# Turning a convolution filter by whole transposes with half-zero tables in a fused gated mixer kernel

## The chip, the core and the metric

The kernel runs on one core of a Trainium2 chip. The metric is the device time of one execution in microseconds (us); the median over the runs is given, with the lowest and the highest. Engines are named as in the profile: PE is TensorE (matmul, and PEld its weight loads), DVE is VectorE, ACT is ScalarE, POOL is GpSimd, and SP issues most DMA transfers.

## The reference

All inputs are bf16; the length S is 2048 and the width D is 640. Two branches of x (which is also q) are mixed by a gate:

```python
def _A_ref(q, k, v, shift_k, ssm_k, ssm_D):      # q, k, v: (1, 2048, 640)
    k_shift = sum over t of k_pad[:, t:t + S, :] * shift_k[:, 3 - t]     # 4 taps
    kv = k_shift * v
    y = irfft(rfft(kv padded to 4096) * rfft(ssm_k padded to 4096))[:2048]
    y = y + kv * ssm_D
    return q * y

def _B_ref(x, w1, w2, w3, w4):
    h = gelu(layernorm(x) @ w1)                  # 640 -> 640
    hs = (four column groups of h, moved by +1, -1, +2, -2 rows) @ w2
    x1 = x + hs
    return x1 + gelu(layernorm(x1) @ w3) @ w4    # 640 -> 1536 -> 640

g = sigmoid((x * gate_w).sum(-1))
return g * _A_ref(x, ...) + (1 - g) * _B_ref(x, ...)
```

## The kernel before

Time is tiled into 16 blocks of 128 rows (NT), the width into 5 blocks of 128 columns (DC). The long convolution is a Fourier transform of length 4096, done in steps of small matmuls against sine tables that the kernel computes itself.

*Branch A.* k is loaded (k_load, `kn`), turned by PE (L571, tile `pst`) and convolved with the four taps by matmuls (tap, L543, tile `psk`). v is gathered by row with indirect DMAs that POOL issues (v_load, L150, four chunks of four blocks, v3 to v0). DVE multiplies both into `KV` (L557 straight from PSUM, L554 from an ACT copy). The filter ssm_k (640 x 2048) is loaded with channels on partitions (load_h, L163, tiles `E` and `HN`) and has to be turned so that time lies on partitions: h_transpose (L343 to L361) does that with PE transposes (L352), two of 128 x 64 for each 128 x 128 tile, one for the even rows of an order "(t2 r t1)" and one for the odd ones (r), at the two column positions of the array. In such a transpose the filter tile is the weight of the matmul, so that its strided view is what PE loads as weights (PEld). One evacuation per 8 tiles writes the turned filter, HT0.

step1 (L378) is the first step of the transform, for KV and for HT0: 4 chunks of 5 units, each unit two matmuls against table F1, one on partitions 0 to 63 and one on 64 to 127 (row positions 0 and 64), 512 columns each. Each unit leaves two PSUM banks, which ACT or DVE copies to `stg` (evac, L325 on ACT and L327 on DVE); SP sends them to DRAM (S_x for KV, S_h for the filter). gather (L396) reads them back in the order of the next step; step2 (L417) does it, product multiplies the two spectra on DVE, step3 (L464) goes back, its results `gs` travel through DRAM (S_g) and gin (L489), and step4 (L829) ends the transform. The gated mix with q (L836, L839) and with branch B (L843) is done there.

*Branch B.* x_stats (L621 and on: DVE statistics at L638, POOL's power at L610 for the reciprocal root, L611) and x_norm (L617) normalise; mlp1 (L663, tile `psm`), h_shift, w2 (L740), x1_norm with a transposing DMA (L767), w3 (L788) and w4 (L806, L808) are the two perceptrons.

*Order.* Nothing is left to a scheduler: a list ORDER of steps (name, arguments, number of the step) is written out by hand, and each engine and queue gets its instructions in that order. Letters in an entry (AAVAAAAVAA) say for each evacuation whether ACT (A) or DVE (V) does it. PSUM banks with tag "c" rotate through 4 buffers, staging rows (tag "row") through 4. warm (L198 to L202) runs 11 matmuls on zeros at the very start. f1_table, f4_table, t2_table and i_tables make the sine tables on DVE with one ACT sine each (L240 to L242).

Of the kernel before, what the change touches and what calls it, by code (L numbers as in the profile page):

```python
# [41 lines left out]
def kernel(  # L42
# [38 lines left out]

    ROWS = const.tile([P, 1], I32, name="ROWS")
    WZ = const.tile([P, 512], BF16, name="WZ")
    IDB = const.tile([P, P], BF16, name="IDB")
    F1 = const.tile([P, H, 2], BF16, name="F1")
    F4 = const.tile([P, 2, H, 2], BF16, name="F4")
# [52 lines left out]
    def col(i):  # L139
        return sm[:, i:i + 1]  # L140
# [57 lines left out]
    def warm():  # L198
        V.memset(WZ[:], 0.0)
        ps = psc.tile([P, 512], F32, name="psz", tag="c")  # L200
        for i in range(11):
            PE.matmul(ps[:], lhsT=WZ[:, 0:P], rhs=WZ[:], start=True, stop=True)  # L202

# [40 lines left out]
    def f1_table():  # L244


        stt(pf2[:], bit(6), -64.0, pf[:])
        ts(col(29), pf2[:], 2.0)
        n = tab([P, H, 2], "n")
        ts(n[:, :, 0], R64[:, 0:H], col(29), pf2[:])  # L250
        ts(n[:, :, 1], n[:, :, 0], float(128 + 128), op0=ALU.add)
        ts(n[:, :, 0], n[:, :, 0], float(64 + 128), op0=ALU.add)
        yield from sin_table(F1[:], n, 256)

# [85 lines left out]
    def h_transpose(dc, ev):  # L340
        if "HT0" not in st:
            st["HT0"] = main.tile([P, NT * D], BF16, name="HT0", tag="RT")
        hv = st.pop(("HN", dc)).rearrange("p (t2 r t1) -> p t1 r t2", r=2, t1=NT)  # L343
        dst = st["HT0"][:].rearrange("p (t d) -> p t d", t=NT)
        def make(hh):
            box = {}

            def first():
                ps = box["ps"] = psc.tile([P, 8, P], BF16, name="pst", tag="c")
                for i in range(8):  # L350
                    for r in range(2):
                        PE.transpose(out=ps[HALF[r], i, :], in_=hv[:, 8 * hh + i, r, :], identity=IDB[:], tile_position=(0, H * r))  # L352
# [13 lines left out]
    def step1(name, c, ev):  # L366
# [5 lines left out]
        def make(u):  # L372
            ps = []

            def first():
                for r in range(2):
                    ps.append(psc.tile([P, 512], F32, name="ps1", tag="c"))
                    PE.matmul(ps[r][:], lhsT=F1[HALF[r]].rearrange("p a b -> p (a b)"), rhs=src[HALF[r], o + 512 * u:o + 512 * u + 512], start=True, stop=True,  # L378
                              tile_position=(H * r, 0))
# [435 lines left out]
    def step4(t1, ev):  # L815
# [32 lines left out]
        "open.L1.left:0 open.A2.right:0 kv_alloc:0 warm:0 load_x0.0:0 consts0:0 load_x0.1:0 k_load.3.AAA:0 load_cj:0 "  # L848
        "consts0:1 f4_table:0 f1_table:0 k_load.1.AAV:0 k_load.2.AAA:0 f4_table:1 f1_table:1 load_x.1:0 k_load.0.AAA:0 "
        "x_stats.0.VVVA:0 x_stats.0.VVVA:1 x_stats.0.VVVA:2 x_stats.0.VVVA:3 x_stats.0.VVVA:4 row_order:0 load_w1:0 "  # L850
        "k_load.3.AAA:5 load_gw:0 k_load.3.AAA:6 k_load.3.AAA:3 k_load.3.AAA:1 k_load.1.AAV:1 k_load.1.AAV:5 "
        "x_stats.0.VVVA:5 k_load.3.AAA:4 k_load.1.AAV:3 load_x.3:0 k_load.3.AAA:2 k_load.1.AAV:2 kv_consts:0 "
        "k_load.2.AAA:3 v_load.3:0 k_load.1.AAV:4 x_stats.0.VVVA:6 x_norm.0.VVVV:0 x_norm.0.VVVV:1 x_norm.0.VVVV:2 "
        "k_load.1.AAV:6 k_load.2.AAA:1 k_load.2.AAA:4 k_load.2.AAA:2 d_fold:0 x_turn.0.VAV:0 x_norm.0.VVVV:3 "
        "x_turn.0.VAV:4 v_load.2:0 k_load.2.AAA:5 x_turn.0.VAV:1 x_turn.0.VAV:2 k_load.2.AAA:6 x_turn.0.VAV:3 "
        "x_turn.0.VAV:5 tap.7.AA:0 tap.7.AA:1 k_load.0.AAA:1 k_wrap:0 tap.9.VA:0 x_stats.1.VVVV:0 x_stats.1.VVVV:1 "
        "x_stats.1.VVVV:2 x_stats.1.VVVV:3 tap.9.VA:1 tap.7.AA:3 k_load.0.AAA:2 load_h.0:0 tap.7.AA:4 x_stats.1.VVVV:4 "
        "k_load.0.AAA:5 tap.9.VA:3 mlp1.0.1:0 tap.5.AV:0 v_load.1:0 x_stats.1.VVVV:5 tap.9.VA:2 k_load.0.AAA:6 "
        "load_x.2:0 tap.7.AA:2 tap.5.AV:3 tap.5.AV:4 mlp1.0.1:1 w1_mixed:0 tap.5.AV:1 tap.6.VA:0 tap.6.VA:1 tap.6.VA:2 "
        "tap.8.VA:0 k_load.0.AAA:3 tap.5.AV:2 mlp1.0.0:0 load_h.1:0 x_norm.1.VVVV:0 x_norm.1.VVVV:1 x_norm.1.VVVV:2 "  # L860
        "x_norm.1.VVVV:3 x_stats.3.VVAA:0 x_stats.3.VVAA:1 tap.6.VA:3 v_load.0:0 tap.8.VA:1 x_stats.3.VVAA:2 "
        "x_turn.1.AAV:4 tap.8.VA:3 x_stats.3.VVAA:3 k_load.0.AAA:4 x_turn.1.AAV:2 x_turn.1.AAV:5 x_turn.1.AAV:0 "
        "x_stats.3.VVAA:4 mlp1.0.2:0 x_stats.3.VVAA:5 x_stats.3.VVAA:6 tap.8.VA:4 x_stats.3.VVAA:7 x_turn.1.AAV:3 "
        "tap.8.VA:2 tap.4.AV:0 tap.6.VA:4 x_turn.1.AAV:1 mlp1.0.0:1 tap.4.AV:1 tap.9.VA:4 x_norm.3.VVVV:0 tap.4.AV:3 "
        "x_norm.3.VVVV:1 tap.4.AV:4 x_norm.3.VVVV:2 tap.3.AA:0 mlp1.0.2:1 x_norm.3.VVVV:3 tap.3.AA:1 mlp1.1.1:0 "
        "tap.3.AA:3 step1.KV.3.VAVAVAAAAA:0 x_stats.2.VVAA:0 step1.KV.3.VAVAVAAAAA:1 step1.KV.3.VAVAVAAAAA:6 "
        "x_stats.2.VVAA:1 x_stats.2.VVAA:2 x_stats.2.VVAA:3 step1.KV.3.VAVAVAAAAA:2 step1.KV.3.VAVAVAAAAA:7 mlp1.1.0:0 "
        "tap.3.AA:4 step1.KV.3.VAVAVAAAAA:8 x_stats.2.VVAA:4 x_stats.2.VVAA:5 tap.0.VV:0 x_stats.2.VVAA:6 x_turn.3.D:0 "
        "tap.4.AV:2 tap.0.VV:3 tap.0.VV:1 mlp1.1.0:1 load_h.3:0 tap.2.AA:0 mlp1.1.1:1 x_stats.2.VVAA:7 tap.0.VV:4 "
        "mlp1.1.2:0 tap.0.VV:2 x_norm.2.VVVA:0 tap.2.AA:3 step1.KV.3.VAVAVAAAAA:3 x_norm.2.VVVA:1 x_norm.2.VVVA:2 "  # L870
        "tap.2.AA:1 step1.KV.3.VAVAVAAAAA:4 x_norm.2.VVVA:3 h_shift.0:0 step1.KV.3.VAVAVAAAAA:5 "
        "step1.KV.3.VAVAVAAAAA:9 step1.KV.3.VAVAVAAAAA:11 mlp1.1.2:1 mlp1.3.0:0 t2_table:0 step1.KV.3.VAVAVAAAAA:10 "
        "tap.2.AA:4 step1.KV.3.VAVAVAAAAA:12 step1.KV.3.VAVAVAAAAA:13 h_shift.0:1 mlp1.3.0:1 tap.1.VV:0 mlp1.3.2:0 "
        "tap.1.VV:1 h_shift.0:2 x_turn.2.D:0 step1.KV.3.VAVAVAAAAA:14 tap.2.AA:2 step1.KV.3.VAVAVAAAAA:16 mlp1.3.1:0 "
        "step1.KV.2.VAAVVAAVAV:6 tap.1.VV:3 tap.1.VV:2 mlp1.3.2:1 step1.KV.2.VAAVVAAVAV:8 tap.1.VV:4 "
        "step1.KV.3.VAVAVAAAAA:15 tap.3.AA:2 step1.KV.2.VAAVVAAVAV:3 step1.KV.2.VAAVVAAVAV:4 t2_table:1 mlp1.2.1:0 "
        "step1.KV.2.VAAVVAAVAV:5 step1.KV.2.VAAVVAAVAV:7 step1.KV.1.AVVAVVAAVA:9 mlp1.3.1:1 step1.KV.1.AVVAVVAAVA:11 "
        "h_shift.1:0 step1.KV.1.AVVAVVAAVA:6 h_shift.0:3 step1.KV.1.AVVAVVAAVA:8 mlp1.2.2:0 step1.KV.1.AVVAVVAAVA:10 "
        "mlp1.2.1:1 load_w2:0 step1.KV.1.AVVAVVAAVA:0 step1.KV.1.AVVAVVAAVA:1 load_h.2:0 h_shift.3:0 h_shift.3:1 "
        "step1.KV.1.AVVAVVAAVA:7 z_rows:0 h_shift.1:1 step1.KV.1.AVVAVVAAVA:12 step1.KV.1.AVVAVVAAVA:2 mlp1.2.0:0 "  # L880
        "mlp1.2.2:1 z_rows:1 step1.KV.1.AVVAVVAAVA:14 step1.KV.1.AVVAVVAAVA:13 step1.KV.1.AVVAVVAAVA:3 "
        "step1.KV.1.AVVAVVAAVA:5 h_shift.3:2 z_rows:2 h_shift.2:0 step1.KV.2.VAAVVAAVAV:9 h_shift.1:2 "
        "step1.KV.1.AVVAVVAAVA:4 step1.KV.2.VAAVVAAVAV:10 w2.0:0 h_shift.2:1 step1.KV.2.VAAVVAAVAV:11 "
        "step1.KV.2.VAAVVAAVAV:0 w2.0:1 mlp1.2.0:1 step1.KV.2.VAAVVAAVAV:12 step1.KV.2.VAAVVAAVAV:13 "
        "step1.KV.2.VAAVVAAVAV:1 h_shift.2:2 w2.15:0 h_transpose.0.VV:2 h_shift.1:3 h_transpose.2.AV:2 "
        "step1.KV.2.VAAVVAAVAV:2 t2_table:2 h_transpose.1.VA:2 step1.KV.2.VAAVVAAVAV:14 h_transpose.0.VV:3 "
        "h_transpose.2.AV:3 w2.15:1 h_transpose.1.VA:0 h_transpose.2.AV:0 h_transpose.2.AV:1 h_transpose.1.VA:1 "
        "h_transpose.0.VV:0 w2.2:0 step1.KV.0.AAAAVAAAAA:0 step1.KV.1.AVVAVVAAVA:16 h_transpose.1.VA:3 "
        "step1.KV.1.AVVAVVAAVA:15 h_transpose.0.VV:1 step1.KV.0.AAAAVAAAAA:1 step1.KV.0.AAAAVAAAAA:6 h_shift.3:3 "
        "load_h.4:0 step1.KV.0.AAAAVAAAAA:8 w2.2:1 step1.KV.0.AAAAVAAAAA:7 step1.KV.0.AAAAVAAAAA:2 w2.12:0 "  # L890
        "step1.KV.0.AAAAVAAAAA:12 w2.2:2 step1.KV.2.VAAVVAAVAV:15 step1.KV.0.AAAAVAAAAA:9 step1.KV.0.AAAAVAAAAA:10 "
        "t2_table:3 t2_table:4 step1.KV.0.AAAAVAAAAA:11 w2.1:0 w2.12:1 step1.KV.0.AAAAVAAAAA:13 "
        "step1.KV.0.AAAAVAAAAA:14 step1.KV.0.AAAAVAAAAA:3 h_shift.2:3 step1.KV.0.AAAAVAAAAA:5 step1.KV.2.VAAVVAAVAV:16 "
        "step1.KV.0.AAAAVAAAAA:4 h_transpose.4.AV:0 h_transpose.4.AV:2 h_transpose.4.AV:3 h_transpose.3.AV:0 "
        "h_transpose.4.AV:1 h_transpose.3.AV:2 z_cols:0 load_w3:0 w2.1:1 h_transpose.3.AV:3 h_transpose.3.AV:1 "
# [159 lines left out]
```

## Time and profile before

| what | value |
|---|---|
| median of 3 runs (lowest to highest) | 241.19 us (241.0 to 242.49) |
| span of the profiled execution | 240.6 us |
| its mean granted TensorE clock | 0.984 |
| PE busy | 227.9 us |
| DVE busy | 193.3 us |
| ACT busy | 170.4 us |
| POOL busy | 19.1 us |
| traffic | 57.08 MB, of which 54.10 MB on SP's queue |

The span goes from the first to the last instruction of one profiled execution, so a sum made from its rows is compared with 240.6 and not with the median. In lists of groups a line reads: line of the kernel, engine, operation, output and inputs by the program's names, and the number of instructions; durations there are of single instructions, and matmuls overlap their successors. How far apart they follow each other is read from the chain of waits, whose lines are: start, length, engine and what it did, and how many instructions.

### The profile page before, as it was taken

Reading aid. Unit: us, or ns where it says so; the run is one execution under the profiler, and the core shown is the slowest. Engines: PE = TensorE matmul, PEld = TensorE weight load, DVE = VectorE, ACT = ScalarE, POOL = GpSimd, SP = SyncE. Lnnn points to the kernel's source line nnn. Section 1 sums busy time; section 2 is a strip of 40 time slices with the busy share of each in tenths; the row PEclk is TensorE's granted clock in tenths of the full one; section 3 lists DMA queues with packets and bytes.
Section 4 is the critical chain, followed back from the end, with each engine's and each line's share of the span. In section 5 each row is a group of like instructions: output and inputs, shape, how many; then the busy total and the mean of one; then the engine's idle time right before and its main releaser. Section 6 shows DMA issues by size and latency. Waiting matters only on the chain.

```text
span 240.6 us, 5764 instructions
## 1 busy us (share of the span) xinstructions
PE 227.9 (95%) x2328; PEld 117.7 (49%) x2328; DVE 193.3 (80%) x449; ACT 170.4 (71%) x303; POOL 19.1 (8%) x32
## 2 busy tenths in 40 slices
PE   6598999999999999999999999999999999989991
PEld 2585755433858445344355334444444345446660
DVE  7876999988876999756679999867688999209994
ACT  4689999779587899899577677675598533436530
POOL 3540322000000020002200300000000000000000
PEclk9689999999999999999999999999999999999999
DMA  6999608693989889994989936199830127689674
GB/s 218 389 379 417 224 2 198 163 343 121 348 302 344 207 346 277 374 385 170 291 206 271 207 121 223 34 244 392 318 110 3 48 107 259 214 301 347 147 276 165
DMA packets 42744, 57.08 MB, mean 237 GB/s; under 512 B 20313, under 2 KB 35418, under 8 KB 42462
## 3 DMA queue, kind: packets, MB, share of 16 engines
q1 hardware_dynamic: 42142, 54.10, 68.5%
q0 software_dynamic: 576, 2.62, 2.9%
q8 instruction: 18, 0.29, 0.5%
q14 instruction: 8, 0.07, 0.1%
HBM read 34.42 MB, written 18.36 MB: 219 GB/s over the span
## 4 chain that ended last, share of the span: by engine, by line
PE 74%; DMA 13%; DVE 9%; POOL 2%; issue 1%; SPq 0%; DVEq 0%
PE ps L788 20%; PE ps L806 15%; PE psw L740 10%; PE psm L663 8%; PE ps L378 5%; PE ps L417 4%; DMA KV<-in_A_v_dram,ROWS 4%; PE pst L352 4%; PE ps L464 3%; PE psk L543 3%; DMA ax<-S_h 2%; DMA q<-in_A_q_dram 2%; DMA gin<-S_g 2%; DVE X L843 2%; DVE q L839 2%; POOL RS L610 2%
## 5 line engine op out<-in xcount | busy, mean ns | idle before, releaser
L806 PE MATMUL ps<-W,gt 128*128 128x512 bf16 (+1 forms) x384 | 56.6, 300 | 0.0
L788 PE MATMUL ps<-x1t,W 128*128 128x512 bf16 x240 | 55.6, 380 | 0.0
L806 PEld LDWEIGHTS <-gt 128*128 128x128 bf16 x384 | 29.0, 98 | 24.9 <-issue 4.6
L788 PEld LDWEIGHTS <-W 128*128 128x128 bf16 x240 | 21.8, 98 | 29.2 <-issue 5.6
L325 ACT CAST stg<-ps 128x512 bf16<-128x512 f32 x51 | 27.3, 597 | 6.7 <-PE ps L378 5.8
L793 ACT ACTIVATE gt<-ps 128x1024 bf16<-128x1024 f32 x24 | 24.8, 1031 | 6.4 <-PE ps L788 6.1
L325 ACT CAST gs<-ps 128x320 bf16<-128x320 f32 x36 | 13.9, 431 | 16.7 <-PE ps L464 11.7
L663 PE MATMUL psm<-xt,WA 128*128 128x512 bf16 x100 | 23.5, 380 | 0.0
L740 PE MATMUL psw<-WA,HT 128*128 128x512 bf16 (+1 forms) x116 | 21.5, 300 | 0.0
L327 DVE CAST stg<-ps 128x512 bf16<-128x512 f32 x29 | 19.3, 683 | 2.5 <-PE ps L378 1.9
L325 ACT CAST hs<-ps 128x512 bf16<-128x512 f32 x28 | 15.2, 591 | 8.3 <-PE ps L417 8.2
L327 DVE CAST gs<-ps 128x320 bf16<-128x320 f32 x28 | 12.7, 485 | 5.6 <-PE ps L464 3.8
L833 ACT ACTIVATE y<-ps,GS 128x320 bf16<-128x320 f32 x19 | 9.7, 526 | 10.0 <-PE ps L829 8.5
L327 DVE CAST XS<-ps 128x512 bf16<-128x512 f32 x18 | 11.8, 684 | 5.7 <-PE ps L417 5.7
L808 DVE SCALAR_TENSOR_TENSOR X<-ps,OMG,X 128x640 bf16<-128x640 f32 x16 | 14.0, 877 | 1.7 <-PE ps L806 1.7
L839 DVE SCALAR_TENSOR_TENSOR q<-ps,GS,q 128x320 bf16<-128x320 f32 x13 | 7.1, 546 | 9.7 <-PE ps L829 9.7
L325 ACT CAST XS<-ps 128x512 bf16<-128x512 f32 x22 | 11.9, 593 | 4.0 <-PE ps L417 3.7
L740 PEld LDWEIGHTS <-HT 128*128 128x128 bf16 x116 | 9.3, 98 | 11.2 <-issue 3.0
L663 PEld LDWEIGHTS <-WA 128*128 128x128 bf16 x100 | 9.0, 98 | 11.5 <-issue 1.6
L742 DVE SCALAR_TENSOR_TENSOR X<-psw,X 128x640 bf16<-128x640 f32 x16 | 12.9, 818 | 0.9 <-PE psw L740 0.7
L417 PE MATMUL ps<-ax,CMP 64*32 64x512 bf16 (+3 forms) x512 | 13.0, 300 | 0.5 <-DMA ax<-S_h 0.5
L745 ACT ACTIVATE jk<-X 128x640 bf16<-128x640 bf16 x16 | 12.0, 751 | 0.0
(141 smaller groups left out, 356.0 us busy)
## 6 DMA issues: line engine op xcount, KB each, us to landing
S_x<-stg SPq DMA_DIRECT2D x8, 640.0 KB
ax<-S_x SPq DMA_DIRECT2D x8, 640.0 KB
S_h<-stg SPq DMA_DIRECT2D x8, 640.0 KB
ax<-S_h SPq DMA_DIRECT2D x8, 640.0 KB
S_g<-gs SPq DMA_DIRECT2D x8, 640.0 KB
W<-in_B_w_dram SPq DMA_DIRECT2D x2, 1920.0 KB
kn<-in_A_k_dram SPq DMA_DIRECT2D x4, 640.0 KB
q<-in_A_q_dram SPq DMA_DIRECT2D x4, 640.0 KB
```

The costliest lines, as they stand in the source:

```text
L325: A.copy(out=dst, in_=src)
L327: V.tensor_copy(out=dst, in_=src)
L378: PE.matmul(ps[r][:], lhsT=F1[HALF[r]].rearrange("p a b -> p (a b)"), rhs=src[HALF[r], o + 512 * u:o + 512 * u + 512], start=True, stop=Tr ...
L417: PE.matmul(ps[j][q:q + 32, lo - 512 * u:hi - 512 * u], lhsT=CMP[HALF[j], 8 * b + 4 * h + i, c, :], rhs=st[name, 2 * b + h][HALF[j], i, lo ...
L663: PE.matmul(ps[:, v, :].rearrange("p (a b) -> p a b", a=4), lhsT=W1N[:, k, 160 * f:160 * f + P] if f < 4 else W1M[:, k, :], rhs=xt[:, :, k ...
L740: PE.matmul(ps[:, o:o + w], lhsT=h_tile(f, t1), rhs=W2P[:, f, o:o + w], start=(f == 0), stop=(f == 4))
L742: V.scalar_tensor_tensor(out=X1[:, t1, :], in0=ps[:], scalar=1.0, in1=X[:, t1, :], op0=ALU.mult, op1=ALU.add, accum_out=S12[:, 0, t1:t1 + 1])
L745: A.activation(out=jk[:], in_=X1[:, t1, :], func=ACT.Square, accum_out=S12[:, 1, t1:t1 + 1])
L788: PE.matmul(ps[:, u, :].rearrange("p (a b) -> p a b", a=4), lhsT=st["W3"][:, k, f * P:(f + 1) * P], rhs=xt[:, :, k, :], start=(k == 0), st ...
L793: A.activation(out=gt[:, 2 * (fp % 2):2 * (fp % 2) + 2, :], in_=ps[:], func=ACT.Gelu_apprx_tanh)
L806: PE.matmul(ps[:, o:o + w], lhsT=st["gt", c, f // 4][:, f % 4, i * P:(i + 1) * P], rhs=st["W4"][:, f, o:o + w], start=(f == 0), stop=(f == ...
L808: V.scalar_tensor_tensor(out=X1[:, t1, :], in0=ps[:], scalar=OMG[:, t1:t1 + 1], in1=X1[:, t1, :], op0=ALU.mult, op1=ALU.add)
```

## The change

1. h_transpose reads the filter in plain row order, "(q t1)", and turns each 128 x 128 tile with one whole transpose: 80 instead of 160.
2. For HT0, step1 uses full 128-row matmuls with a new table F1N, which has two versions: one with the odd rows' entries zero and one with the even rows'. KV keeps F1 and its halves.
3. f1n_table makes F1N: one sine as for F1, then a multiplication by a 0/1 column and a subtraction. f1_table moves to a later place.
4. warm issues 11 matmuls at the start as before, and 4 times 3 more, placed between the k transposes. Its moving operand is a broadcast 128 x 128 tile.
5. pow0 runs one POOL power on constants early.
6. The v loads: v3 was issued near the start, v2 and v1 behind the first x_stats power, v0 behind the second. Now v3 and v2 go behind the first and v1 and v0 behind the second.
7. ORDER is new throughout, and so are the letters of the evacuations. Among the loads on SP: before X0a, X0b, k3, shift_k, k1, k2, x1, k0, w1, gate_w, x3, D, h0, x2, h1, ...; after X0a, X0b, k3, k1, k2, k0, shift_k, x1, w1, x3, gate_w, x2, D, h0, h3, and then, behind the transposing DMAs and the first S_x sends, h1 and h2. Counts, DVE and ACT, before to after: stg 29/51 to 35/45, gs 28/36 to 21/43, XS 18/22 to 16/24, step4's gated product (L839) 13 to 9 on DVE with y on ACT 19 to 23. Just ahead of the last S_g transfer two evacuations of gs stand on DVE before, three after.

```diff
+    PW = const.tile([P, 8], F32, name="PW")
-    WZ = const.tile([P, 512], BF16, name="WZ")
+    WZ = const.tile([P, P], BF16, name="WZ")
+    F1N = const.tile([P, 2, H, 2], BF16, name="F1N")
...
     def warm():
         V.memset(WZ[:], 0.0)
         ps = psc.tile([P, 512], F32, name="psz", tag="c")
-        for i in range(11):
-            PE.matmul(ps[:], lhsT=WZ[:, 0:P], rhs=WZ[:], start=True, stop=True)
+        for n in (11, 3, 3, 3, 3):
+            for i in range(n):
+                PE.matmul(ps[:].rearrange("p (a b) -> p a b", a=4), lhsT=WZ[:], rhs=WZ[:].unsqueeze(1).to_broadcast([P, 4, P]), start=True, stop=True)
+            yield
+
+    def pow0():
+        G.memset(PW[:], 1.0)
+        G.tensor_tensor(out=PW[:, 0:4], in0=PW[:, 0:4], in1=PW[:, 4:8], op=ALU.pow)
...
+    def f1n_table():
+        ts(col(27), bit(0), -1.0, pf[:], op1=ALU.add)
+        ts(col(28), col(27), 0.5)
+        n = tab([P, H, 2], "n")
+        ts(n[:, :, 0], R64[:, 0:H], col(27), col(28))
+        ts(n[:, :, 1], n[:, :, 0], float(128 + 128), op0=ALU.add)
+        ts(n[:, :, 0], n[:, :, 0], float(64 + 128), op0=ALU.add)
+        yield from sin_table(F1N[:, 0], n, 256)
+        yield
+        V.tensor_scalar(out=F1N[:, 1], in0=F1N[:, 0], scalar1=bit(0), scalar2=None, op0=ALU.mult)
+        V.tensor_tensor(out=F1N[:, 0], in0=F1N[:, 0], in1=F1N[:, 1], op=ALU.subtract)
...
     def h_transpose(dc, ev):
-        hv = st.pop(("HN", dc)).rearrange("p (t2 r t1) -> p t1 r t2", r=2, t1=NT)
+        hv = st.pop(("HN", dc)).rearrange("p (q t1) -> p t1 q", t1=NT)
...
                 for i in range(8):
-                    for r in range(2):
-                        PE.transpose(out=ps[HALF[r], i, :], in_=hv[:, 8 * hh + i, r, :], identity=IDB[:], tile_position=(0, H * r))
+                    PE.transpose(out=ps[:, i, :], in_=hv[:, 8 * hh + i, :], identity=IDB[:])
...
     def step1(name, c, ev):
...
-                    PE.matmul(ps[r][:], lhsT=F1[HALF[r]].rearrange("p a b -> p (a b)"), rhs=src[HALF[r], o + 512 * u:o + 512 * u + 512], start=True, stop=True,
-                              tile_position=(H * r, 0))
+                    if name == "HT0":
+                        PE.matmul(ps[r][:], lhsT=F1N[:, r].rearrange("p a b -> p (a b)"), rhs=src[:, o + 512 * u:o + 512 * u + 512], start=True, stop=True)
+                    else:
+                        PE.matmul(ps[r][:], lhsT=F1[HALF[r]].rearrange("p a b -> p (a b)"), rhs=src[HALF[r], o + 512 * u:o + 512 * u + 512], start=True, stop=True,
+                                  tile_position=(H * r, 0))
...
     ORDER = (
...
-        "x_stats.0.VVVA:5 k_load.3.AAA:4 k_load.1.AAV:3 load_x.3:0 k_load.3.AAA:2 k_load.1.AAV:2 kv_consts:0 "
-        "k_load.2.AAA:3 v_load.3:0 k_load.1.AAV:4 x_stats.0.VVVA:6 x_norm.0.VVVV:0 x_norm.0.VVVV:1 x_norm.0.VVVV:2 "
...
+        "k_load.2.AAA:0 k_load.3.AAA:4 x_stats.0.VVVA:4 pow0:0 k_load.1.AVA:1 f1n_table:0 k_load.1.AVA:6 "
+        "x_stats.0.VVVA:5 k_load.0.AAA:0 k_load.1.AVA:2 load_cj:0 load_x.1:0 k_load.1.AVA:3 k_load.2.AAA:3 row_order:0 "
+        "x_stats.0.VVVA:6 load_w1:0 warm:3 k_load.2.AAA:4 k_load.2.AAA:5 warm:4 v_load.3:0 v_load.2:0 f1_table:0 "
...
```

## The prediction

> **What bounds the kernel now.** I read the head of the page first, then the waits of TensorE (PE), then the windows of the first 80 us, the chain of waits there, and last the views of the tiles pst, E, kn and xn.
>
> ```profile
> PE 227.9 (95%) x2328; PEld 117.7 (49%) x2328; DVE 193.3 (80%) x449; ACT 170.4 (71%) x303; POOL 19.1 (8%) x32
> ...
> PE 74%; DMA 13%; DVE 9%; POOL 2%; issue 1%; SPq 0%; DVEq 0%
> ```
>
> PE is busy for 95% of the span and holds 74% of the chain. A PE microsecond saved is therefore worth about one microsecond, as long as DVE and ACT can follow. The waits of PE show how little else there is:
>
> ```profile
> PE pst L571 <- DMA kn<-in_A_k_dram: 3.3, 2, 2.6
> PE psk L543 <- DVE KV L557: 1.2, 1, 1.2
> PE psz L202 <- DVE NPI L213: 1.2, 1, 1.2
> PE ps L829 <- DMA gin<-S_g: 0.8, 1, 0.8
> PE ps L417 <- DMA ax<-S_h: 0.5, 1, 0.5
> ```
>
> All large ones lie in the first 25 us. The windows show that from 25 us on PE has no gap, and how near DVE is to being the bound there:
>
> ```profile
> core 0: us, PE busy (x) PEld busy (x) DVE busy (x) ACT busy (x) POOL busy (x), PEclk, DMA share, GB/s
> ...
> 10.00:15.00 5.00, 4.36 (x46) 4.16 (x44) 3.77 (x6) 4.13 (x6) 4.46 (x4) 0.56 1.01 412
> ...
> 20.00:25.00 5.00, 3.79 (x49) 2.27 (x49) 3.25 (x11) 4.46 (x7) 1.13 (x2) 1.00 1.02 416
> 25.00:30.00 5.00, 5.00 (x70) 3.70 (x66) 4.93 (x15) 4.53 (x10) 1.19 (x2) 1.00 0.58 191
> ...
> 60.00:70.00 10.00, 10.00 (x127) 7.53 (x126) 7.63 (x16) 6.42 (x9) 0.00 (x0) 1.00 0.92 311
> ```
>
> DVE is 96% busy from 25 to 50 us (4.93, 4.84, 4.48, 4.85 and 4.87 of each 5), and 76% from 60 to 80. The chain says what sets the start of the gapless stretch (start, length, what):
>
> ```profile
> 8.76 3.71 POOL RS L610
> ...
> 12.90 10.10 DMA KV<-in_A_v_dram,ROWS
> ...
> 23.13 0.42 DVE KV L554
> ...
> 24.35 1.99 PE psk L543 x38
> ...
> 29.05 1.12 PE pst L571 x20
> ...
> 33.11 2.26 PE psm L663 x10
> 35.37 0.54 PE ps L378 x4
> ```
>
> The POOL power (L610) takes 3.71 us, the two v loads queued behind it take 10.1 us to land, and only then can KV be multiplied and PE go on. Finally the transposes, by tile:
>
> ```profile
> L352 PE MATMUL pst<-IDB,E x96: 273/274/323, 61.6 to 66.9; 128*64 128x128 bf16 x96
> L571 PE MATMUL pst<-IDB,kn x80: 219/314/314, 7.8 to 26.7; 128*128 128x128 bf16 x80
> L571 PE MATMUL pst<-IDB,xn x40: 216/219/219, 14.5 to 29.9; 128*128 128x128 bf16 x40
> ```
>
> **Part by part, against the profiled 240.6 us (the median, 241.19, is 0.6 above; I add that at the end).**
>
> *Filter transposes.* The chain holds them as two pieces, 96 halves in 5.50 us and 64 in 3.71 us: 9.21 us, or 115 ns for each pair of halves. After, 80 whole ones take the place of the 80 pairs. The nearest whole transpose is L571, 20 in 1.12 us, or 56 ns each: 80 x 56 = 4.5 us, a gain of 4.7. But its weights (xn) lie side by side, and the filter's are strided: every 16th element after, every 32nd before. A strided load of 64 columns (tile E's weight rows: 204 ns) lasts twice one of 128 packed columns (xn's: 98). So the pair before is likely set by its loads, not by its matmuls. If a strided column keeps its price, the whole transpose loads as many columns as the pair, and takes the pair's 115 ns: gain 0. If one load does not share the work as the pair's two at once do, 128 columns would cost twice the pair, 230 ns: 18.4 us, a loss of 9.2. Low end -4.7, high end +9.2, with 0 between. I take -4.7, since operation, shape and type are those of L571 and the stride is halved, but with little over even odds among the three.
>
> The row above (204 against 98) is where the Trainium skill can be weighed. "TensorEngine Tiling (Array Packing)", section "Restrictions", says that column tiling switches Fast Weight Load off; "TensorE: Matmul & The Clock Gate", section "Weight-path perf modes", says that Fast Weight Load is on for 128 bf16 columns, strided ones included. By these the slow load belongs to the halves, and the sum goes with -4.7. "SBUF — State Buffer", section "Door 1: The DMA port swizzle", speaks against: its 16-byte lines cost a penalty at each crossing, and a step of 16 bf16 still crosses one per column, which would leave the sum at 0. The trace has no whole strided load, so neither is shown here.
>
> *First DFT step of the filter.* 20 units. Before, a unit is two 64-row matmuls running together: four of them, two units, in 0.54 us, 0.27 a unit. After, two full matmuls one behind the other; L663 x10 (full rows, 512 columns) takes 2.26, 0.226 each, 0.453 a unit. 20 x (0.453 - 0.27) = +3.7 us, all on PE and all in its gapless stretch. This has one answer; the evacuations keep number and size.
>
> *Start of the KV stage.* RS waits only for the statistics. With the power warmed up by the early dummy (pow0, on POOL while it would be idle), RS should take what its later runs take, 1.06 to 1.12 us: 2.6 us earlier. Before RS, DVE gets f1n_table (its small rows: 0.15 + 0.15 + 0.32 + 0.43 + 0.23 = 1.3 us) but f1_table (the same rows, 1.3) moves behind it: even. f1n's last two operations, about 0.2 each, come to 0.4 and lie in DVE's slack before 20 us. pow0 would cost something only if it ran past RS's input: it stands ahead of RS on POOL, which is idle for 5.29 us there, and 3.71 fits if it starts before 5 us. The v loads: v2 and v1 were issued at 12.90 and landed at 23.0. Now v3 and v2 go at 12.90 - 2.6 = 10.3; the same 10.1 us brings them to 20.4. v3 no longer lands early, at 10.3, but nothing used it before 23. DVE then needs its x_stats.1, which ended at 21.45 before, and PE would go on at some 22.3 instead of 24.35: -2.0. Low end -2.6 (all of RS). High end: +1.0, if the loads that follow (v1 and v0, now behind the second RS; before, v1 was with v2 and landed at 23) come behind taps 3 and 4: issued at about 23.5 and 24.5 they land some 5 to 10 us later (5.0 is the shortest row, 10.1 the longest), while DVE reaches their products some 8 us on. I take -2.0.
>
> *Longer warm-up.* 12 more matmuls of 0.37 to 0.4 us at the cold clock (11 take 3.8 us), 2.6 at full clock (0.22 each): 2.6 to 4.8 us of PE. They go between the k transposes, where PE waits 3.3 us for kn, and before the restart at 24 us, where it idles 2.1. The granted clock is 0.76 and 0.56 from 5 to 15 us; L571 on kn is 314 there against 219 on xn. If they hold it at 1.0, the kn transposes get faster by a third. All of it ends before v lands: 0. Without that cover up to +2 us.
>
> *DVE in the new order.* Letters change, so that by the end of the filter's first step DVE has some 6 us more behind it (the KV units four more evacuations of 0.68 = 2.7, f1n 1.7, the rest x and filter units); it gives this back behind 130 us, in step3 and step4 (seven 0.485 and four 0.55 fewer). From the first KV product to the last group of filter transposes DVE has some 43.5 us of work for 47.5 of PE, 92%, where it had 42.2 in 47. With PE pulled in by 4.7 in that stretch some evacuations come late: 0 to +2.5, and I take +0.9 from the 96% it has already reached in 25 to 50 without stopping PE.
>
> *The middle and the tail.* PE's list from 100 to 205 us has the same matmuls, and the gathers of S_h, of which the one at 120 cost 0.5, are issued in a like place: 0 (-0.5 to +0.7). In the last part three gs evacuations instead of two stand on DVE ahead of the S_g transfer (+0.47, so that the 0.8 wait for gin becomes 1.2), and step4 has four fewer gated products on DVE, which is 19.5 of 20 us busy from 216 to 236: 0 (-0.9 to +0.5).
>
> Sum: 240.6 - 4.7 + 3.7 - 2.0 + 0.9 = 238.5, and with 0.6 for the median **239.1 us**.
>
> **The rivals.**
>
> *A. The stride, not the half, is what costs (other side).* Place: h_transpose. If a strided column keeps its load price, the 80 transposes stay at 9.2 us while the first step pays 3.7: 239.1 + 4.7 = 243.8. For: 204 ns for 64 strided against 98 for 128 packed columns, and each matmul of a half (274) is longer than a whole one's (219). Against: the step is halved. It decides from 75 ns per transpose on: 80 x 75 = 6.0, where the sum meets 240.6. If a single load does not share the work (230 ns) the time is near 253; one chance in twenty.
>
> *B. DVE becomes the bound from 22 to 75 us.* PE finishes its transposes early and waits for evacuations and KV products; the whole net gain of the transposes and half the ramp goes: about 241.2. For: 96% in 25 to 50. Against: DVE idles 24% from 60 to 80, where the transposes stand.
>
> *C. The start gains nothing.* v lands beside k, x, w1 and h loads (DMA share 1.0 from 10 to 25 us) and its first use stays at 23 to 24 us: 241.1. For: two loads side by side took 10.1 us, twice the single row of 5.0. Against: fewer bytes are in front.
>
> *D. More than forecast.* Faster k transposes and the lighter DVE in the tail count too: -1.9: 237.2.
>
> **How the numbers follow.** Forecast (237.8 to 240.2) 0.38, A 0.27 (of which 0.05 the worst form), B 0.14, C 0.10, D 0.11. A measurement of this kernel tells about 1% from no change: 238.8 and 243.6 are the edges. Faster: 0.25 of the forecast's 0.38, and D: 0.36. Slower: half of A's 0.22 (0.11), its worst form (0.05), and 0.08 of B and C, where the new order may cost more than I put down: 0.24. Same: 0.40. The range reaches from D to A with the ramp lost (243.8 + 1.5): 236.9 to 245.3. With both signs open, the forecast's own range stands beside it.
>
> **What would show it.** Right: the filter's transposes as whole pieces of 56 ns in the chain, 4.5 us in all, and the filter's L378 successor at 0.45 a unit; RS at 1.1 us; PE going on after the first KV product at about 22.3; from there no PE wait on DVE above 1 us. Wrong: whole weight loads of E above 150 ns with transposes of 100 or more (A), PE waits on stg, psk or KV between 25 and 80 us (B), PE restarting at 24 (C), or a wait for S_g above 2 us at the end.

## The result, and the profile after

The changed kernel takes 244.38 us (median of 20 runs, 241.98 to 245.61), the kernel before 241.56 in the same comparison (20 runs, 240.5 to 244.45). The ratio is 1.0101, with an interval of 1.0073 to 1.0129: 1% slower, some 2.4 us. The profiled execution spans 242.1 us and took 243.83; in every run listed the time is 1.7 to 1.9 us above the span.

The page after, head and chain:

```profile
PE 226.2 (93%) x2242; PEld 116.6 (48%) x2260; DVE 192.9 (80%) x453; ACT 174.0 (72%) x313; POOL 17.0 (7%) x34
...
PE 61%; DMA 15%; DVE 14%; ACT 4%; issue 3%; POOL 1%; SPq 1%; DVEq 0%
```

PE is busy 1.7 us less (18 of its matmuls have no record in this trace: 2242 against 2260 weight loads). Its share of the chain falls from 74% to 61%, and DMA, DVE and ACT take over. The waits of PE (total, times, longest) and the windows of the start show where:

```profile
PE pst L595 <- DMA kn<-in_A_k_dram: 3.2, 1, 3.2
PE ps L853 <- DMA gin<-S_g: 1.0, 2, 0.9
PE psz L205 <- DVE NPI L222: 1.0, 1, 1.0
PE ps L402 <- DVE stg L349: 1.0, 1, 1.0
PE ps L441 <- DMA ax<-S_h: 0.9, 1, 0.9
PE psk L567 <- ACT xt L347: 0.7, 1, 0.7
PE psk L567 <- DVE KV L581: 0.7, 1, 0.7
```

```profile
10.00:15.00 5.00, 5.00 (x51) 3.62 (x50) 1.26 (x2) 4.05 (x5) 2.30 (x4) 0.82 1.06 375
15.00:20.00 5.00, 4.01 (x68) 3.37 (x67) 5.00 (x8) 4.90 (x7) 0.00 (x0) 1.00 1.04 392
20.00:25.00 5.00, 4.57 (x63) 2.87 (x58) 4.83 (x17) 4.88 (x8) 0.00 (x0) 1.00 0.88 330
25.00:30.00 5.00, 4.54 (x61) 3.38 (x61) 4.97 (x16) 4.38 (x11) 3.05 (x4) 1.00 0.15 36
```

DVE (third busy column) does 1.26 us of work from 10 to 15 us, where it did 3.77 before, and is then full. The DMA engines (share, second last column) are nearly idle from 25 to 30 us, at 0.15 instead of 0.58: what was issued has landed, POOL issues the second pair of v loads at 28.0 and 29.3, and SP's next transfer follows at 37.6. The chain (start, length, what):

```profile
13.46 1.81 ACT KT L347 x2
...
24.55 0.68 DVE KV L581
...
26.41 1.15 POOL RS L634
...
29.30 6.05 DMA KV<-in_A_v_dram,ROWS
...
57.24 0.70 DVE stg L349
...
64.63 3.00 PE pst L373 x48
...
73.39 2.14 PE pst L373 x32
...
76.92 0.86 PE ps L400 x4
```

The first KV product starts at 24.55 instead of 23.13. It does not wait for v: v3 and v2, issued at 10.46 and 11.93, took 8.7 and 10.1 us and had landed at 19.2 and 22.0. DVE is late: its statistics of x's second chunk (x_stats.1) end at 24.26 (before: 21.45), and the table's last two rows, 0.20 and 0.23 us, stand between them and the product. From there to 57.9 the chain is mostly DVE, with POOL and the third and fourth v load from 26.4 to 35.4.

The first w2 matmul of branch B starts at 61.1 instead of 58.1. (Both lists have almost the same entries ahead of it, the table and the warm-up aside.) Of these 3.0 us 1.4 are there at the first KV product in this profile (in e4 and e13 below, whose lists are the same up to there, it starts at 22.84 and 23.98; in e1, which has the old list up to there, at 21.34); from it to the first w2 the changed kernel takes 36.5 us instead of 35.0, with DVE busy for 33.9 instead of 33.0. Behind that point the changed kernel is not slower: 242.1 - 61.1 = 181.0 us against 240.6 - 58.1 = 182.5. The transposes are what the forecast took: 3.00 + 2.14 = 5.1 us instead of 9.2. Their tile rows:

```profile
L373 PEld LDWEIGHTS <-E x48: 146/148/156, 64.4 to 67.3; 128*128 128x128 bf16 x48
L373 PE MATMUL pst<-IDB,E x48: 224/226/233, 64.5 to 67.4; 128*128 128x128 bf16 x48
```

### The profile page after: what moved, and what is told of

Its sections match the earlier page's. It is cut to its first block, busy times and chain, and to the rows that moved or that the text cites. A ratio compares the mean times of both kernels' runs of the same rounds, so it can differ in the third digit from the quotient of the medians.

```text
span 242.1 us, 5619 instructions
## 1 busy us (share of the span) xinstructions
PE 226.2 (93%) x2242; PEld 116.6 (48%) x2260; DVE 192.9 (80%) x453; ACT 174.0 (72%) x313; POOL 17.0 (7%) x34
## 4 chain that ended last, share of the span: by engine, by line
PE 61%; DMA 15%; DVE 14%; ACT 4%; issue 3%; POOL 1%; SPq 1%; DVEq 0%
PE ps L830 16%; PE ps L812 16%; PE psw L764 8%; DMA S_h<-stg 4%; PE ps L441 3%; PE ps L400 3%; DMA kn<-in_A_k_dram 3%; PE ps L488 3%; DMA ax<-S_h 3%; DMA KV<-in_A_v_dram,ROWS 2%; PE ps L853 2%; PE pst L373 2%; PE psm L687 2%; DVE stg L349 2%; ACT KT L347 2%
## 5 line engine op out<-in xcount | busy, mean ns | idle before, releaser
L830 PE MATMUL ps<-W,gt 128*128 128x128 bf16 (+1 forms) x371 | 55.2, 297 | 0.8 <-issue 0.3
L347 ACT CAST stg<-ps 128x512 bf16<-128x512 f32 x45 | 24.4, 592 | 6.7 <-PE ps L402 3.6
L347 ACT CAST gs<-ps 128x320 bf16<-128x320 f32 x43 | 15.8, 435 | 16.3 <-PE ps L488 8.4
L349 DVE CAST stg<-ps 128x512 bf16<-128x512 f32 x35 | 22.9, 684 | 3.0 <-PE ps L402 1.6
L764 PE MATMUL psw<-WA,HT 128*128 128x512 bf16 (+1 forms) x111 | 20.6, 296 | 0.2
L857 ACT ACTIVATE y<-ps,GS 128x320 bf16<-128x320 f32 x23 | 11.4, 526 | 8.7 <-PE ps L853 7.4
L349 DVE CAST gs<-ps 128x320 bf16<-128x320 f32 x21 | 9.4, 486 | 7.4 <-PE ps L488 6.8
L349 DVE CAST XS<-ps 128x512 bf16<-128x512 f32 x16 | 10.5, 686 | 5.7 <-PE ps L441 5.7
L349 DVE CAST hs<-ps 128x512 bf16<-128x512 f32 x13 | 9.0, 689 | 7.5 <-PE ps L441 7.4
L441 PE MATMUL ps<-ax,CMP 64*32 64x256 bf16 (+3 forms) x512 | 13.3, 300 | 0.9 <-DMA ax<-S_h 0.9
L863 DVE SCALAR_TENSOR_TENSOR q<-ps,GS,q 128x320 bf16<-128x320 f32 x9 | 4.8, 550 | 9.7 <-PE ps L853 8.4
```

The source lines that it names most:

```text
L347: A.copy(out=dst, in_=src)
L349: V.tensor_copy(out=dst, in_=src)
L441: PE.matmul(ps[j][q:q + 32, lo - 512 * u:hi - 512 * u], lhsT=CMP[HALF[j], 8 * b + 4 * h + i, c, :], rhs=st[name, 2 * b + h][HALF[j], i, lo ...
L764: PE.matmul(ps[:, o:o + w], lhsT=h_tile(f, t1), rhs=W2P[:, f, o:o + w], start=(f == 0), stop=(f == 4))
L830: PE.matmul(ps[:, o:o + w], lhsT=st["gt", c, f // 4][:, f % 4, i * P:(i + 1) * P], rhs=st["W4"][:, f, o:o + w], start=(f == 0), stop=(f == ...
L857: A.activation(out=box["y"][:], in_=box["ps"][:], func=ACT.Copy, scale=GS[:, t1:t1 + 1])
```

## The experiments

Theory S, formed from this profile: the filter part gains what PE's rows say, and the loss is DVE's late start. DVE's own waits in the changed kernel, 8 to 62 us, gave the first suspect; the KT copy it waits to make (k1's second group) stands ahead of xn, which was ready at 10.3 us:

```profile
DVE KT L349 <- PE pst L595: 3.7, 1, 3.7
DVE stg L349 <- PE ps L402: 0.9, 1, 0.9
DVE KV L581 <- DMA KV<-in_A_v_dram,ROWS: 0.6, 1, 0.6
```

Ratios below are to the kernel before, timed together with it on the same chip, with 95% intervals; the changed kernel stands at 1.0101 [1.0073, 1.0129].

**The filter part alone, in the kernel before (e1, e8, e11).** The three differ only in the table:

```diff
+ whole transposes, F1N, full matmuls in step1 for HT0
  e1:  f1n_table between the steps of t2_table (60 to 75 us)
  e8:  f1n_table behind x_stats.1 (20.5 us), sine before the first gelu
  e11: def f1n_table(): G.memset(F1N[:], 0.01); yield; yield
```

> The kernel before with only the filter part of the change: whole transposes, F1N, full matmuls in its first step; f1n_table is made at 60 to 75 us, where DVE has slack. Theory S (the loss is in the first 60 us, where DVE is held up; the filter part gains): the transposes give 4.1 us (9.21 to 5.14 in the chains), the first step takes 3.2, so 0.5 to 1.5 us faster than before, ratio 0.994 to 0.998. Rival F (the filter part is what costs, its full matmuls and later evacuations): 1 to 3 us slower, ratio 1.004 to 1.012.

> As the filter part alone, but with f1n_table where DVE waits for v (21.45 to 23.13) and its sine beside work that needs no new table, so that the 1.2 us for which PE waited at 63 behind f1n's rows is gone. If that placing was the cost: 0 to 1 us faster than before. If the filter part costs by itself (evacuations of HT and stg come late once the transposes are short, and S_h is gathered later): again 1 to 2.5 us slower, ratio 1.004 to 1.010.

> The kernel before with the filter part (whole transposes, full matmuls in the first step) but without the table's computation (F1N filled with a constant by POOL, so the filter's spectrum is not computed). Theory T: what is left is PE's own account, 9.21 to some 5.2 us for the transposes and 3.2 us more for the first step: 0 to 1.5 us faster than before, ratio 0.994 to 1.000. Rival F (evacuations and later transfers eat it): 1 to 3 us slower, as with the table.

e1: 1.0106 [1.0047, 1.0164]. e8: 1.0171 [1.0115, 1.0228]. e11, which leaves the table's computation out and so has a wrong filter spectrum: 1.0024 [0.9979, 1.0069]. So S's first half was wrong: with its table the filter part is slower in the old list. Without the table no cost can be measured, but no gain either: PE's rows (-4.1 and +3.2, together -0.9 us, a ratio of 0.996) lie just below e11's interval, so part of that gain is lost.

By the ratios the table is worth 0.8%, some 2.0 us, in e1 (its interval overlaps e11's) and 1.5%, some 3.6, in e8, for some 1.7 us of DVE work and a sine. The profiles show it as waiting. In e8 ACT stands idle for 3.8 us in front of the sine, until DVE has made its input at 21.96; ACT's copies of k and the first gelu behind it come late (25.54 instead of 22.16), and PE waits 2.7 us for KV. The first w2 group starts at 60.6 instead of 58.1. In e1 the loss lies behind the first w2 matmul, which starts at 57.6: from it to the end 185.2 us instead of 182.5, with DVE waiting 1.8 us for the sine and PE 2.0 us for copies by DVE.

**The filter part undone in the changed kernel (e4).**

```diff
- transpose(out=ps[:, i, :], in_=hv[:, 8 * hh + i, :]), F1N in step1
+ the half transposes and F1's pairs of before, in the new ORDER; F1N is still made
```

> The changed kernel with half transposes in the old row order and F1's pairs of 64-row matmuls in the filter's first step again; f1n_table is still made and not used. Theory S: 0.5 to 1.5 us slower than the changed kernel, 245 to 246. Rival F: 1 to 3 us faster, 241.5 to 243.5.

1.0146 [1.0085, 1.0207]: not faster, and not clearly slower than the changed kernel. So nothing shows the whole transposes and full matmuls as what costs in the new list; the table is made in both.

**The table left out of the changed kernel (e9), the KT copy moved (e3), both (e10), the warm-up out (e2).**

```diff
  e9:  f1n_table as in e11
  e3:  ... f1_table:0 [k_load.1.AVA:4 moved] ... kv_consts:0 k_load.1.AVA:4 ...
  e2:  -for n in (11, 3, 3, 3, 3):  +for n in (11, 0, 0, 0, 0):
```

> The changed kernel with f1n_table's computation left out: one POOL memset fills F1N with a constant, so the filter's spectrum is not computed. DVE loses 1.3 us of rows ahead of 8.1 us and 0.43 at 24.2, ACT one sine of 0.4. Theory T (the table's time on DVE is dear, because DVE's list is full from 14 to 58 us): 0.5 to 1.5 us faster than the changed kernel (244.4), mostly by the 0.43 and by what the sine holds up, since the first 1.3 us are covered by DVE's stop from 10.1 to 13.9. Rival: under 0.3 us, all of it hidden.

> The changed kernel with one entry moved: DVE's copy of k1's second group of transposes (KT) stands behind xn and DG instead of ahead of them, so that DVE does not sit idle from 10.1 to 13.9 us with xn ready at 10.3. Theory S: DVE's list, which is busy from 13.9 to 58 us without a gap, starts up to 3.7 us earlier, bounded by v's landing at 20.6 to 22: 2 to 3.5 us faster than the changed kernel, 241 to 242.4. Rival V (the later v loads, not this copy, set the pace from 24 to 36 us): under 1 us.

> The changed kernel with f1n_table's computation left out as in the run before (F1N filled with a constant) and DVE's KT copy behind DG. Theory T: with the stop at 10.1 to 13.9 us gone too, both parts count: 2 to 3 us faster than the changed kernel, 241.4 to 242.4, so about as long as the kernel before. If the rest of the new order is what costs: 243 or more.

> The changed kernel without the 12 later warm-up matmuls; all else is the same. Theory S, in the form that the warm-up matmuls delay the k transposes on which DVE's KT copy at 13.9 us waits: the 9 or so that run ahead of it or between take 3.7 us at the half clock, the transposes then run at 314 instead of 219 ns (some 56 to 110 ns apart), so DVE goes on 0.5 to 2 us earlier, and the kernel is 0.5 to 2 us faster than the changed one: 242.5 to 244 where the changed one has 244.4. Rival W (the warm-up is what keeps the clock, its loss costs more): 0 to 2 us slower than the changed one.

e9: 1.0055 [1.0008, 1.0102]; e3: 1.0089 [1.0052, 1.0125]; e10: 1.0082 [1.0043, 1.0121]; e2: 1.0112 [1.0066, 1.0158]. Only e9's ratio moves much, by about half of the loss, and its interval still overlaps the changed kernel's. e10 beside e3 makes the same change, the table left out, and gains 0.0007. Moving the copy did remove the stop, but DVE's list then met the next one, the load of shift_k that the new order puts behind k0. DVE's waits in e3:

```profile
DVE DG L527 <- DMA cr<-in_A_shift_k_dram: 1.5, 1, 1.5
DVE stg L349 <- PE ps L402: 0.9, 1, 0.9
DVE KV L581 <- DMA KV<-in_A_v_dram,ROWS: 0.6, 1, 0.6
```

**The start, part by part, in the kernel before (e5, e6, e7, e12, e15).**

```diff
  e5:  v_load.3:0 +pow0:0
  e6:  kv_consts:0 (DG) moved behind x_norm.0.VVVV:2
  e12: as e6, and load_w1:0 ahead of k_load.0's load
  e7:  +warm:1 .. warm:4 between the k transposes
  e15: v_load.3:0 moved to v_load.2:0, v_load.1:0 moved to v_load.0:0
```

> The kernel before with the early dummy power alone, on POOL between the first v load and the first real power. The prediction's theory (the first power is long because it is the first): RS falls from 3.71 to about 1.1 us, v2 and v1 are issued 2.6 us earlier, and the kernel is 1 to 2 us faster. Rival P (in the changed kernel the dummy itself, the first power of all, took 1.03 us at 1.88; RS was long before because DVE's 2.83 us multiplication DG ran from 8.73 to 11.56 beside it, and the changed kernel moves DG to 16.11): RS stays at 3.7, time within 0.5 us of before.

> The kernel before with DG's multiplication moved on DVE from ahead of x chunk 0's normalisation to behind its third xn; nothing else. Rival P: RS takes 1.0 to 1.1 us instead of 3.7, v2 and v1 are issued at 10.3 instead of 12.9 and land near 20.5 instead of 23.0; DVE idles 1.5 us in front of xn, then loses 1.7 us of waiting for v: 0.5 to 2 us faster than before. The prediction's theory: RS stays at 3.7 and the move costs DVE its cover, so 0 to 3 us slower.

e5: 1.0033 [0.9999, 1.0067]; e6: 1.0009 [0.997, 1.0048]. Here are POOL's rows and DVE's DG in the kernel before, in e5 and in e6 (start, length, engine, line):

```profile
8.73 2.83 DVE L503 TENSOR_TENSOR DG<-IDB,cr 128x2560 bf16<-128x2560 bf16 x1
...
8.76 3.71 POOL L610 TENSOR_TENSOR RS<-VE,EXPO 128x4 f32<-128x4 f32 x1 [5.29 <-DVE VE L648]
12.54 0.21 POOL L611 TENSOR_TENSOR NB<-MU,RS 128x4 f32<-128x4 f32 x1
```

```profile
8.84 2.83 DVE L509 TENSOR_TENSOR DG<-IDB,cr 128x2560 bf16<-128x2560 bf16 x1 [0.17 <-DMA cr<-in_A_shift_k_dram]
...
8.75 1.02 POOL L616 TENSOR_TENSOR RS<-VE,EXPO 128x4 f32<-128x4 f32 x1 [3.95 <-DVE VE L654]
9.84 1.87 POOL L617 TENSOR_TENSOR NB<-MU,RS 128x4 f32<-128x4 f32 x1
```

```profile
11.31 2.81 DVE L503 TENSOR_TENSOR DG<-IDB,cr 128x2560 bf16<-128x2560 bf16 x1
...
8.77 1.05 POOL L610 TENSOR_TENSOR RS<-VE,EXPO 128x4 f32<-128x4 f32 x1 [5.29 <-DVE VE L648]
...
11.57 3.36 POOL L150 DMA_INDIRECT KV<-in_A_v_dram,ROWS  x1 [0.30 <-issue]
```

Each time the long instruction on POOL is the one that starts while DVE's DG runs (8.73 to 11.56 before, 8.84 to 11.67 in e5, 11.31 to 14.12 in e6). In the kernel before it is RS; in e5 DG began 0.1 us later, RS got through in 1.02 and NB took 1.87 instead of 0.21; in e6 DG stands behind xn, RS takes 1.05 and the issue of the second v load 3.36 instead of 0.94. So it is the neighbour that makes RS long, not that it is the first: rival P. (In e5 the dummy came first and RS was short, as the prediction's theory has it; but that theory gives no reason for NB's 1.87, nor for e6, which has no dummy.) e1 and e7 have no dummy either: there DG happened to start late, at 9.32 and 9.35, waiting for shift_k, RS took 1.05 and NB 2.31 and 2.34. And the earlier v brings nothing: in e6 the first KV product starts at 20.6, but PE then waits for w1, whose transfer shares the DMA engines with v:

```profile
PE pst L571 <- DMA kn<-in_A_k_dram: 3.3, 2, 2.0
PE psm L663 <- DMA WA<-in_B_w_dram: 1.8, 1, 1.8
```

> The kernel before with DG behind xn and, on SP, w1's load ahead of k0's instead of behind it. With DG later alone PE waited 1.8 us for w1, from 19.5 to 21.3, and the time was that of before. If the transfers' order was what swallowed the gain: w1 lands 1.5 us earlier, PE goes on at 19.7 and the kernel is 1 to 2 us faster than before. If the first 25 us are bound by the sum of all transfers (the DMA engines are full from 10 to 25 us), k0 or v is late instead: within 0.7 us of before.

> The kernel before with the 12 later warm-up matmuls alone, three behind each of the four groups of k transposes in which the changed kernel has them. Theory S: the matmuls take 3 to 4.5 us of PE at 8 to 16 us, the transposes are quicker by 0.1 us each at most; v's landing at 23.0 still ends the wait of DVE, so it is within 0.7 us of before. Rival W (warm-up delays the k copies and with them DVE): 1 to 2.5 us slower.

> The kernel before with only the later v: v3 issued with v2 behind the first power, v1 and v0 behind the second. Theory D: v2 and v3 land at 23 as v2 and v1 did, k and x come 1 us earlier without v3 beside them; v1 and v0, issued at 25.3 and 26.5, land at 31 to 33, where DVE wants them at 31 to 38: within 0.7 us of before, ratio 0.997 to 1.003. Rival V: 1 to 3 us slower, ratio 1.004 to 1.012.

e12: 1.0088 [1.0043, 1.0132]: with w1 ahead, k0 is what comes late (PE waits 2.6 us for it at 19.8, and 6.5 in all for kn, before 3.3). e7: 1.0022 [0.9987, 1.0058]: no cost of the warm-up can be measured. e15: 1.0175 [1.0133, 1.0217]: the later v alone costs 3 to 5 us. DVE's waits from 15 to 60 us in e15 begin with

```profile
DVE KV L554 <- DMA KV<-in_A_v_dram,ROWS: 5.0, 1, 5.0
```

and the first w2 group starts at 61.8.

**Letters and v, undone in the changed kernel (e13, e14).**

```diff
  e13: -step1.KV.3.AAAVVVAVAV .2.VVAAAVAVAA .1.AVVAAAVVVV .0.VAVAAAAAAA
       +step1.KV.3.VAVAVAAAAA .2.VAAVVAAVAV .1.AVVAVVAAVA .0.AAAAVAAAAA
  e14: v_load.3:0 moved behind row_order:0, v_load.1:0 behind v_load.2:0
```

> The changed kernel with the letters of the KV units' evacuations as in the kernel before, by unit and half: 14 on DVE instead of 17, the rest on ACT. Theory D (DVE has 2.9 us more to do ahead of the first w2 group than before, 61.8 against 58.9, and it is the engine without a gap there): 2 us less on DVE, 1 to 2 us faster than the changed kernel, ratio to before 1.002 to 1.006. Rival (ACT is as full from 30 to 45 us, and the list was written for these letters): within 0.7 us of the changed kernel, or slower.

> The changed kernel with the v loads issued as before: v3 at some 3 us, v2 and v1 behind the first power, v0 behind the second. Theory D: v made DVE wait 0.64 us only (v1, at 35.4), so within 0.7 us of the changed kernel. Rival V (late v is a cost of its own: v1 and v0 are issued at 28.0 and 29.3 and land 6 us later): 1 to 2.5 us faster than the changed kernel, ratio to before 1.000 to 1.006.

e13: 1.0152 [1.0098, 1.0206]: theory D (DVE has too much to do ahead of the first w2 group) does not hold in this form, though what e13 takes from DVE goes to ACT, which is as full from 30 to 40 us. e14: 1.0142 [1.0082, 1.0202]: early v does not help the new list either, since w1 is then late. Its PE waits begin with

```profile
PE psm L687 <- DMA WA<-in_B_w_dram: 3.1, 1, 3.1
```

**Several repairs together (e16 to e18).**

```diff
  e16: e2 + e3, and load_cj:0 right behind k_load.3's load
  e17: e16 + e9
  e18: e17 + e14
```

> The changed kernel with three repairs of its start: no later warm-up matmuls, DVE's KT copy behind DG, and shift_k loaded on SP right behind k3 as in the kernel before (with the copy alone moved, DVE waited 1.5 to 2.6 us for shift_k in its place). Theory D (the loss is DVE's late start and its longer list ahead of the first w2 group): DVE goes on at 10.3 without a stop, first KV product at v's landing (21 to 22 instead of 24.5), second power at 23, first w2 group at 58 to 59 instead of 59.1 to 61.1, 1 to 2 us faster than the changed kernel, ratio to before 1.002 to 1.006. If the start is bound otherwise: 1.008 or more.

> The same with f1n_table's computation left out (F1N filled with a constant, so the filter's spectrum is not computed). Theory D: 1.7 us less on DVE, so at the kernel before or under it, ratio 0.996 to 1.002. If it stays at 1.005 or more, the rest of the loss is in neither the table nor the stop nor the warm-up, but in the order of the rest of the list.

> The changed kernel with table, warm-up, KT copy and shift_k as in the run before (F1N filled with a constant, so the filter's spectrum is not computed), and the v loads issued as in the kernel before. Theory D2 (table and late v are the two causes: in the old list the table at the start alone moved the first w2 group from 58.1 to 60.6 us, the late v alone to 61.8): with both out the first w2 group is at 57.5 to 59 and the ratio to before 0.996 to 1.003. Rival (with v early the transfers collide, w1 lands late as in the changed kernel with v early alone, where PE waited 3.1 us for it): 60 us or later, 1.005 or more.

e16: 1.0112 [1.0072, 1.0152]; e17: 1.0107 [1.0063, 1.0152]; e18: 1.0125 [1.0063, 1.0186]. All three contradict what D and D2 expected. In e16 and e17 DVE no longer stops, and waits for v instead (3.1 and 3.4 us). A part of this is rival P again: with the stop gone, DG runs early, and the issue of the second v load starts beside it. In e16:

```profile
11.92 2.82 DVE L527 TENSOR_TENSOR DG<-IDB,cr 128x2560 bf16<-128x2560 bf16 x1
...
12.43 3.12 POOL L152 DMA_INDIRECT KV<-in_A_v_dram,ROWS  x1 [0.30 <-issue]
```

In e17 this issue takes 3.12 us too and in e18 3.40, where the changed kernel's took 0.94. So e16 to e18 removed one hindrance and put another, 2.2 to 2.5 us, in its place; they do not show what the start would take without both. Beside e16, e17 shows again what the table is worth in the new list: 0.0005. In e18 v is there, and the other loads are late:

```profile
PE pst L588 <- DMA kn<-in_A_k_dram: 3.6, 4, 2.1
PE psm L680 <- DMA WA<-in_B_w_dram: 2.0, 1, 2.0
```

Where branch B's first w2 matmul starts, from one profile each (us):

| kernel | first w2 |
|---|---|
| before; e5, e6, e7, e12 (its start varied) | 58.1; 58.8, 58.4, 57.2, 58.7 |
| e1, e11 (filter, no table in the start) | 57.6, 58.1 |
| e8 (table in the start), e15 (late v) | 60.6, 61.8 |
| after; e2, e3, e9, e10 (one or two parts undone) | 61.1; 59.1, 59.8, 60.3, 60.6 |
| e4, e13 (filter part, letters undone) | 59.4, 62.3 |
| e14, e16, e17, e18 | 63.3, 61.4, 59.7, 62.3 |

The old list is at 57.2 to 58.8 unless the table or the late v is put into its start. The new list is at 59.1 to 63.3, whatever part of it is undone. From there to the end all but three profiles take 180.4 to 182.8 us; e1 takes 185.2, e4 186.0, e13 184.3. One profile is a rough measure: the first k transpose alone starts anywhere from 6.3 to 8.7 us (before 7.8, after 8.7). No variant was measurably faster than the kernel before.

## Why the prediction was wrong, point by point

*Filter transposes: -4.7 forecast, -4.1 measured.* 62 to 67 ns each: 3.00 and 2.14 us instead of 9.21. Rival A's condition (75 ns) did not occur. A strided whole load does take longer in the records, 148 ns against 98 for a packed one, but the transposes follow each other only 6 to 11 ns further apart than the packed ones (56). Of the two rules of the Trainium skill weighed in the prediction, the one on tiling and Fast Weight Load ("TensorEngine Tiling (Array Packing)", "Restrictions") fits the time; no run tests the rule by itself. The crossing penalty of the Trainium skill, "SBUF — State Buffer", section "Door 1: The DMA port swizzle", may be in the 148, but it did not leave the sum at 0.

*First DFT step: +3.7 forecast, +3.2 measured.* Two units take 0.86 us instead of 0.54.

*Start of the KV stage: -2.0 forecast; this is the step that failed.* The first links came as forecast: RS fell to 1.01 us, though for another reason than the dummy power, v was issued at 10.46, and had landed at 19.2 and 22.0 (forecast: 20.4). The link that failed is "DVE then needs its x_stats.1, which ended at 21.45 before". It kept the old list's time for a list that was new. DVE sat 3.7 us in front of a copy of k, ran xn, DG and the statistics 2 to 7 us later than before, ended x_stats.1 at 24.26 and made the first product at 24.55. So PE went on at 25.29, not at "some 22.3", and in none of the three profiles with this start did even the first product begin before 22.84. The sum counted the wait that goes and not what is late next.

Taking the stop away did not bring the gain either. From 10 to 25 us the DMA share is 1.0 in the profile of before, which the prediction itself quoted under rival C, and each repair met another late load: w1 (e6, e14, e18), k0 (e12), shift_k (e3, e10) or v (e16, e17, where DG's neighbourhood is part of it). The high end given for v1 and v0, +1.0, was too small for the old list, where the late v alone costs 3 to 5 us; in the changed kernel itself DVE waits 0.6 us for them.

*The table: "even" and 0.4 us "in DVE's slack" forecast; not settled.* In the old list it costs some 2.0 and 3.6 us (e1, e8 beside e11). In the new list the three pairs with and without it differ by 1.1 us (e9), 0.2 (e10 beside e3) and 0.1 (e17 beside e16), none clear of the intervals. Its rows were priced rightly, but the last two were not in slack: they ran at 24.18 to 24.55, right ahead of the first KV product.

*DVE in the new order: +0.9 forecast.* By its rows' lengths DVE has 61.8 us to do ahead of the first w2 group instead of 58.9 (the table 1.6, two more stg copies 1.4, a KT copy 0.55, two h_shift copies 0.56, less other parts). The rows overlap, and by busy time it is 52.7 instead of 50.7. Rival B named this engine and stretch, but put its price at the transposes' gain, and it came earlier and from other work: the loss is whole at the first w2 group, ahead of the transposes. e13 and e17, which took such work off DVE, were not faster, so DVE's load alone is not shown to be the cause.

*Longer warm-up, middle and tail: 0 forecast.* e7 and e2 agree for the warm-up, within their intervals. (PE's idle time before its restart, put at 2.1 us, is 1.2 in the rows.) From the first w2 matmul to the end the changed kernel needs 1.5 us less than before, close to the forecast's -1.0.

*The base.* The sum added 0.6 us to a span to get a time. All later runs show 1.7 to 1.9, so the profiled 240.6 belonged to a time of about 242.4, the slowest of the three shown. This shifts the forecast number, not its direction.

What stays open: in the profiles the loss sits ahead of the first w2 group, and the first part of it, 1.4 us in the profile, is DVE's late start. Which part of the change brings the rest is not shown. The late v costs 3 to 5 us alone in the old list, and the table 2.0 to 3.6, but undoing either in the new list gave no clear gain. Why the new list with several repairs is still 1% slower (e16 to e18) is not settled beyond the waits named: v, with DG beside its issue, in two of them, w1 and k in the third. No run kept DG away from the v issues with the stop gone, and none tried a new order of all loads together.

## What to carry to other kernels

Before a wait is counted as gone, look up in the new order when every other input of the same instruction is ready; here v came early and DVE did not. While the DMA engines were full, from 10 to 25 us, an earlier load made another one late (e6, e12, e14), so add up what has to land by when. A small table costs what it makes others wait: in e8 ACT waited 3.8 us for a sine whose DVE rows take 1.3. And a hand-written order belongs to its costs: one part put into the other list, or one taken out, often had a worse ratio than either list whole (e4, e8, e13, e14, e15; only e15's interval is clear of the changed kernel's).

## What the runs showed of the hardware

A POOL instruction that started while DVE's 128x2560 bf16 multiplication (DG, 2.83 us) ran ended only after DG: RS 0.9 us after it (3.71 us long instead of 1.05), NB within 0.1 us (1.87 to 2.34 instead of 0.21), the issue of an indirect load 0.8 us after it (3.12 to 3.40 instead of 0.94). The Trainium skill, "SBUF — State Buffer", section "Terms", says that DVE and GpSimd share a port pair that one holds for its whole instruction. These rows agree. The other way round no run shows it: in e1, e5 and e7 DG started while RS was running, and took its 2.83 us all the same.

The start of the kernel varies by itself: the first k transpose, which waits for k3's load, started between 6.3 and 8.7 us in these profiles, from the same load order ahead of it in each list. This may be part of why single runs of one kernel differ by 3 us and more, and it is why a comparison of many runs decides here.
